# Attention with a threshold, then a two-layer feed-forward: the first nine periods of the schedule rearranged

## The chip, the cores and the metric

One core of a Trainium2 chip runs the whole program. The metric is the device time of one execution in microseconds (us). The kernel before took 487.23 us, the median of three runs (485.38 to 487.64).

## The reference

Eight batches, eight heads, 576 tokens, head size 64. For each head:

```python
scores = scale * np.matmul(q, k.transpose(0, 1, 3, 2))        # scale = 1/8
thresh = np.max(scores, axis=-1, keepdims=True) - tau
scores = np.where(scores >= thresh, scores, -1000000000.0)
attn = np.exp(scores - np.max(scores, axis=-1, keepdims=True))
attn = attn / (np.sum(attn, axis=-1, keepdims=True) + 1e-09)
x = np.matmul(attn, v)                                        # then heads side by side: 4608 x 512
h = x @ w_in                                                  # 512 -> 2048
out = np.maximum(0.01 * h, h) @ w_out                         # 2048 -> 512
```

Because a weight is kept or dropped by comparing its score with the row's maximum less 0.02, scores have to be accurate. The kernel splits each fp32 q and k into two fp16 halves, a high one and the low rest, and forms a score from three fp16 products (high x high, low x high, high x low).

## The kernel before

The work is cut into 72 *periods*. A period is four tiles of 128 queries by 576 keys: four heads of one batch and one of four interleaved blocks of query tokens (m = 0..3), in two sets of heads (so periods 0 and 1 are m = 0 of batch 0, periods 2 and 3 are m = 1, and so on); the 64 tokens left at the end of each batch form tail periods. Batch 1 begins at period 8. The loop `while n < N + PV_LAG` (line 633) writes out one period per turn, by hand: the order of the lines is the order on each engine's queue, and every queue is served in order.

What one turn n does:

- **TensorE (PE)**: `scores` (line 302) forms the four score tiles in PSUM. Then it turns q and k of later periods, turns the reciprocal sums of period n-2 (`spread`), does `pv` of period n-2 (weights times v, line 418), two halves of the feed-forward (`layer1`, `layer2`, lines 456 and 473), with `idle` matmuls in periods 0 to 3 that only keep its clock up.
- **VectorE (DVE)**: `copy_min` (line 336) four times, 0.75 us each by the profile, copies the negated scores to SBUF and takes their minimum; `weights` (line 376) makes the weights of the "plain" tiles; `evacuate` multiplies `pv` by the reciprocal sums into x.
- **ScalarE (ACT)**: `exp_plain` for the plain tiles (one instruction each), `exp_steep` for the others (two each, no work on DVE), the copies out of PSUM and the leaky relu.
- **GpSimd (POOL)**: `split_pool`, three instructions which make the fp16 halves of a pair of heads of q or k, in the period before they are turned; casts of v; DMAs that cast (`load_w` brings w_in in four parts, then w_out in four parts, fp32 to fp16 on the way); from period 5 on also the small loads (`small_at`).
- **SyncE (SP)**: the other DMAs, among them `turn_w` (line 387), a DMA transpose that turns the 128 x 2304 weights of a period for `pv`.

Three things around the change:

- *Weights turned on TensorE.* In the first periods DMA is busy with loads, so `here` (line 637) is true for the weights of periods 0, 1 and 2: in turn n+1 TensorE transposes them in three batches (6, 8 and 4 blocks of 128 columns, `turn_w_here`), and ACT, ACT and DVE copy the batches out (`take_w`). From period 3 on `turn_w` issues a DMA transpose from SP in turn n+1, and `pv` uses it in turn n+2.
- *Two ways for q and k.* The long way: POOL makes the halves (`split_at`), TensorE turns 16 fp16 pieces (`turn`), ACT and DVE copy one bank each (`take`). The short way, `unit32`: TensorE turns the fp32 values themselves, ACT takes the high half out of PSUM (`take_high`) and DVE the low one (`take_low`). Batch 0 goes the short way (its raw tiles, listed in `MIXED`, are loaded in four parts); of batch 1 three units do, in periods 5, 7 and 8.
- *A signal between the row halves.* Two pieces of a score tile pair share a PSUM bank, so one matmul of `scores` waits for a do-nothing instruction that another queue passes on once an earlier matmul is done. `SIGNAL` (line 279) names the queue: POOL in periods 0 and 1, SP in period 2, POOL in 3 to 8, SP from 9. It is queued behind all that this queue was given in the turns before.

`behind_masks` makes POOL's first work of turn n wait for the last `weights` of period n-1. Raw q and k tiles have four buffers, raw v two.

Of the kernel before, what the change touches and what calls it, by code (L numbers as in the profile page):

```python
# [33 lines left out]
def kernel(  # L34
# [10 lines left out]
    nc = tc.nc  # L45
# [30 lines left out]
            out=t[:, :, :], in_=SRC[which][b, ds(4 * s, 4), 0:MAIN, :].rearrange("h (p t) d -> p h (t d)", t=4))  # L76


    MIXED = [(0, 0, "k"), (0, 0, "q"), (0, 1, "k"), (0, 1, "q"), (1, 0, "k"), (1, 1, "q")]

    def load_part(b, s, which, h=None, t=None, eng=None):
        if (b, s, which) not in raws:
# [108 lines left out]
    def unit32(b, which, p0, np=1, t0=0, nt=4):  # L191
        return (b, which, p0, np, t0, nt)
# [64 lines left out]
    periods, first_of = [], []  # L257
# [249 lines left out]
    def at(d, n, f):  # L507
        d.setdefault(n, []).append(f)
# [68 lines left out]
    early32[1] = [[q32[0, 1]]]  # L577
    late32[1] = [q32[0, 2]]
    early32[2] = [[q32[1, 1]]]
    late32[3] = [q32[1, 2]]  # L580
    def load_w_in():

        loads = [load_w(i) for i in range(4)]
# [6 lines left out]
        at(pool_at, 1 + p // 2, lambda p=p: cast_v(0, p))  # L590
    at(pool_at, 1, lambda: cast_vtails(0))
    for i in range(4):
        at(pool_at, 1 if i < 2 else 4, lambda i=i: load_w(4 + i))

    def split_at(n, key):
        at(split_at_, n - 1, key)
# [1 line left out]


    at(loads_at, 0, lambda: load_v(0, 1))  # L600
    at(small_at, 6, lambda small: load_tails(0, "q", small=small))
    split_at(9, (0, "t", "q"))
    in_turn = [(p, w_) for p in range(NP) for w_ in "kq"]
    for b in range(1, B):
        E = 18 * (b // 2)
        if b == 1:
            units = [(0, "k", 4), (0, "q", 5), (1, "q", 6), ("t", "k", 6), (2, "k", 7), (3, "k", 8), ("t", "q", 9)]
            late32[5], late32[7], late32[8] = [unit32(1, "k", 1)], [unit32(1, "q", 2)], [unit32(1, "q", 3)]
            rows, t_at, v_at, casts = (0, 2, 4, 5), (3, 6), (4, 7, 4), (6, 7, 9, 10, 9)
        elif b % 2 == 0:  # L610
            units = [(*u, E - 8 + i) for i, u in enumerate(in_turn)] + [("t", "k", E - 5), ("t", "q", E + 9)]
            rows, t_at, v_at = (E - 11, E - 10, E - 7, E - 6), (E - 8, E + 6), (E - 5, E - 1, E - 4)
            casts = E - 1, E, E + 1, E + 2, E
        else:
            units = [(*u, E + i + i // 4) for i, u in enumerate(in_turn)] + [("t", "k", E + 4), ("t", "q", E + 9)]
            rows, t_at, v_at = (E - 3, E - 2, E + 2, E + 3), (E + 1, E + 6), (E + 1, E + 4, E + 2)
            casts = E + 3, E + 3, E + 6, E + 7, E + 5
        for p, w_, n in units:
            split_at(n, (b, p, w_))
        for i, (s, w_) in enumerate(((0, "k"), (0, "q"), (1, "k"), (1, "q"))):  # L620
            at(loads_at, rows[i], lambda b=b, s=s, w_=w_: load_main(b, s, w_))
        for w_, n in zip("kq", t_at):
            at(small_at, n, lambda b=b, w_=w_, small=nc.sync: load_tails(b, w_, small=small))
        for s in range(2):
            at(loads_at, v_at[s], lambda b=b, s=s: load_v(b, s))
        at(small_at, v_at[2], lambda b=b, small=nc.sync: load_vtails(b, small=small))
        for p in range(NP):
            at(pool_at, casts[p], lambda b=b, p=p: cast_v(b, p))
        at(pool_at, casts[4], lambda b=b: cast_vtails(b))

    N = len(periods)
    n = 0
    while n < N + PV_LAG or l1q or pending or l2q or stores:
        st = periods[n] if n < N else None
        before = periods[n - 1] if 1 <= n <= N else None
        due = periods[n - PV_LAG] if PV_LAG <= n < N + PV_LAG else None
        here = before and before.n < 3
        plain = 2 if n < 2 else 3
        keys, now32, late = turns_at.get(n, []), early32.get(n, []), late32.get(n)


        if n == 0:
            def between():
                copy_min(st, 0)
                copy_min(st, 1)
                take_low(k32[1])
                for x in now32:
                    turn32(x)
            scores(st, between)
            turn32(late)  # L650
        elif st:
            scores(st)
        bank = turn(keys) if keys else None
        for x in now32 if n else []:
            turn32(x)
        if here:
            before.wt = sb.tile([128, 2, 9, 128], FP16, tag="wT", bufs=4, name="wT")
            bank = ps.tile([128, 1024], FP16, tag="h", bufs=2, name="tp")
        if due:
            bank = spread(due, bank)  # L660
        if here:
            turn_w_here(before, 0, 6, bank[:, 0:768])
        for key in keys:
            take(key, 0, on_act)
        if due:
            take_spread(due, bank)
        for x in now32:
            take_high(x)
        if here:
            take_w(before, 0, 6, bank[:, 0:768], on_act)  # L670
        if st:
            copies(st, before, lambda: [take(key, 1, on_dve) for key in keys], now32)
            exp_plain(st, 0)
            if n == 0:
                exp_plain(st, 1)
                take_high(late)
                take_low(late)
        elif before:
            recip(before)
        work = [lambda key=key: split_pool(key) for key in split_at_.get(n, [])] + pool_at.get(n, [])  # L680
        for i, f in enumerate(work):
            mm = f()
            if i == 0 and before:
                behind_masks(mm, before)
        for key in keys:
            if key[1:] == ("t", "k"):
                widen_keys(key[0])
        if n >= 5:

            for f in small_at.get(n, []):  # L690
                f(small=nc.gpsimd)
        if n < 4:
            idle((4, 10, 8, 4)[n], spare("o"))
        if here:
            o = ps.tile([128, 1024], FP16, tag="o", bufs=1, name="wp")
            if n < 3:
                turn_w_here(before, 6, 8, o)
        elif before and st:
            turn_w(before)
        for f in loads_at.get(n, []) + (small_at.get(n, []) if n < 5 else []):  # L700
            f()
        while stores and (n >= N or n not in loads_at or len(stores) > 1):
            store()

        if due and (n == 3 or n > N):
            pv(due)
            if n > N:
                evacuate(due)
        if n == 3:
            turn_w_here(before, 6, 8, o)  # L710
            idle(12, spare("h"))
        for half in range(2):
            if half == 1 and n == 3:
                exp_steep(st, 3)
            for _ in range(2):
                if l2q:
                    layer2()
            if l1q:
                layer1()
            elif n >= N:  # L720
                settle()
            if half == 0:
                if st:
                    for i in range(1, plain if n else 0):
                        exp_plain(st, i)
                if here:
                    take_w(before, 6, 8, o, on_act)
                if late and n not in (0, 3):
                    turn32(late)
                    take_high(late)  # L730
                if n == N:

                    before.wt = sb.tile([128, 2, 9, 128], FP16, tag="wT", bufs=4, name="wT")
                    free = [(sc[:, ts(i, 512)].bitcast(FP16), 8 * i, m) for i, m in enumerate((8, 8, 2))]
                    for o, first, m in free:
                        turn_w_here(before, first, m, o)
                if due and n <= N:
                    if n != 3:
                        pv(due)
                    evacuate(due)  # L740
                if n == N:
                    a, *more = [take_w(before, first, m, o[:, 0 : 128 * m], on_dve if first else on_act)
                                for o, first, m in free]
                    for x in more:
                        tc.declare_no_dep(x.ins, a.ins, reason="other banks")
            elif st and n != 3:
                for i in range(plain, 4):
                    exp_steep(st, i)
        if n == 3:
            turn32(late)  # L750
            take_high(late)
        if here:
            o = ps.tile([128, 512], FP16, tag="o", bufs=1, name="wp")
            turn_w_here(before, 14, 4, o)
        for i in range(plain if st else 0):
            weights(st, i)
            if late and n and i == (2 if n == 3 else 0):
                take_low(late)
            if here and i == 1:
                take_w(before, 14, 4, o, on_dve)  # L760
        n += 1
# [33 lines left out]
```

## Time and profile before

| | |
|---|---|
| median of three runs | 487.23 us (485.38 to 487.64) |
| profiled execution, its own time | 485.95 us |
| its span, first to last instruction | 484.2 us |
| busy share of the span | PE 96%, DVE 89%, ACT 87%, POOL 44% |
| mean granted TensorE clock | 0.996 |
| first score matmul of periods 1 to 10 | 13.79, 21.02, 28.78, 35.50, 42.66, 49.66, 60.66, 67.67, 74.81, 81.08 us |

The difference between a line of the last row and the next is the length of a period. From period 9 on a period takes about 6.3 us, and PE and DVE are busy for all of it; so time lost or won in the first periods is found again at the end of the kernel. Period 5 runs from 42.66 to 49.66 us, period 6 from 49.66 to 60.66 us.

In the profile, "L389" is a line of the kernel; "SPq" or "POOLq" are instructions of a queue that move no data themselves, such as the issue of a DMA. A DMA's time "to landing" is from its issue to its completion signal. Times in the timeline are from the start of the span.

### The profile page before, as it was taken

What the parts mean: (1) busy time and instruction counts of PE and PEld (TensorE: products, weight loads), DVE (VectorE), ACT (ScalarE), POOL (GpSimd) and SP (SyncE); (2) the same over time, 40 slices, a digit from 0 to 9 for tenths busy, and PEclk for the clock granted to TensorE, in tenths of its full rate; (3) what the DMA queues carried; (4) which work ended last, traced back from release to release, by engine and by line L of the source; (5) the groups of instructions that cost most, each with busy time, mean ns of one, the idle gap of its engine ahead of it and who ended that gap; (6) DMA issues with size and microseconds to landing.
All of it is one profiled execution on the core that took longest, in us unless ns stands there. A gap on an engine that the chain in (4) does not pass through costs nothing.

```text
span 484.2 us, 25192 instructions
## 1 busy us (share of the span) xinstructions
PE 465.3 (96%) x10834; PEld 377.4 (78%) x10834; DVE 433.1 (89%) x1311; ACT 420.5 (87%) x781; POOL 215.0 (44%) x353
## 2 busy tenths in 40 slices
PE   7878799999999999999999999999999999999996
PEld 5667688888888888888888778888878788777774
DVE  3988789999999999999999989999999999999940
ACT  4898588999999999999999989999999899988862
POOL 2636545554465464454465574454456473000000
PEclk9999899999999999999999999999999999999999
DMA  9999987799899989789899988979899997655541
GB/s 176 233 218 189 205 189 165 153 187 199 181 177 189 237 168 173 156 164 212 178 189 192 185 188 185 151 180 192 185 184 203 193 184 123 123 122 123 123 95 45
DMA packets 206752, 83.68 MB, mean 173 GB/s; under 512 B 175792, under 2 KB 201392, under 8 KB 206640
## 3 DMA queue, kind: packets, MB, share of 16 engines
q1 hardware_dynamic: 199728, 74.79, 80.1%
q0 software_dynamic: 5504, 6.82, 7.4%
q8 instruction: 85, 1.39, 1.2%
q10 hardware_dynamic: 1408, 0.46, 0.4%
q14 instruction: 27, 0.22, 0.2%
HBM read 36.70 MB, written 9.44 MB: 95 GB/s over the span
## 4 chain that ended last, share of the span: by engine, by line
PE 87%; ACT 6%; DMA 4%; DVE 1%; issue 1%; SPq 0%; POOL 0%; POOLq 0%; ACTq 0%
PE hp L466 25%; PE o L479 25%; PE sc L297 21%; PE pv L426 8%; DMA wT<-w 4%; PE tp L410 3%; PE tp L186 3%; ACT w L373 1%; ACT e L367 1%; ACT s L372 1%; ACT wT L402 1%; PE sc L523 1%; DVE s L338 1%; ACT g L469 1%; ACT qT L232 0%
## 5 line engine op out<-in xcount | busy, mean ns | idle before, releaser
L338 DVE TENSOR_SCALAR_CACHE_REDUCE s<-sc 128x576 f32<-128x576 f32 x288 | 205.3, 753 | 17.4 <-PE sc L297 17.1
L466 PEld LDWEIGHTS <-win 128*64 128x64 f16 x4608 | 147.1, 110 | 28.8 <-DVE xt L437 1.1
L378 DVE SCALAR_TENSOR_TENSOR w<-s,th,e 128x576 f16<-128x576 f32 x214 | 164.4, 815 | 0.6 <-DVE x L445 0.2
L367 ACT ACTIVATE e<-s,mn 128x576 f16<-128x576 f32 x214 | 158.3, 778 | 0.0
L479 PE MATMUL o<-wout,g 128*64 128x512 f16 x1152 | 149.4, 381 | 0.4 <-DMA wout<-in_moe_w_out_dram 0.4
L466 PE MATMUL hp<-x,win 128*64 128x128 f16 x4096 | 137.1, 220 | 0.4 <-DVE kT L249 0.4
L469 ACT ACTIVATE g<-hp 128x512 f16<-128x512 f32 x144 | 86.1, 598 | 44.0 <-PE hp L466 43.9
L297 PE MATMUL sc<-kT,qT 64*128 64x384 f16 (+7 forms) x1920 | 120.5, 284 | 2.4 <-SPq L331 0.9
L297 PEld LDWEIGHTS <-qT 64*128 64x128 f16 (+1 forms) x1920 | 89.8, 97 | 19.7 <-SPq L331 2.0
L160 POOL TENSOR_SCALAR scaled<-raw 128x512 f32<-128x512 f32 x53 | 32.7, 616 | 148.2 <-DVE w L378 128.1
L479 PEld LDWEIGHTS <-g 128*64 128x64 f16 x1152 | 58.6, 110 | 29.6 <-issue 0.7
L171 POOL TENSOR_TENSOR half<-scaled,half 128x512 f16<-128x512 f32 (+1 forms) x68 | 71.7, 1054 | 5.8
L373 ACT ACTIVATE w<-s,minus_tau 128x576 f16<-128x576 f32 x74 | 57.4, 776 | 2.4
L372 ACT ACTIVATE s<-s,th 128x576 f32<-128x576 f32 x74 | 56.8, 767 | 0.7 <-DVE th L356 0.7
L426 PE MATMUL pv<-wT,v 128*64 128x128 f16 (+1 forms) x1600 | 53.0, 214 | 4.0 <-DMA wT<-w 2.8
L426 PEld LDWEIGHTS <-v 128*64 128x64 f16 x1600 | 45.8, 110 | 4.9 <-issue 4.0
L167 POOL CAST half<-scaled 128x512 f16<-128x512 f32 (+1 forms) x68 | 38.2, 562 | 4.4
L445 DVE TENSOR_TENSOR x<-pv,by 128x256 f16<-128x256 f32 x64 | 27.1, 424 | 8.1 <-PE pv L426 6.5
L416 ACT COPY by<-tp 128x256 f16<-128x256 f16 x72 | 26.8, 372 | 1.1 <-PE tp L397 1.1
L186 PEld LDWEIGHTS <-half 64*128 64x128 f16 x968 | 24.4, 95 | 3.5 <-DVE qT L239 1.4
L186 PE MATMUL tp<-ident,half 64*128 64x64 f16 x968 | 24.5, 190 | 1.0 <-DVE qT L239 1.0
L113 POOL CAST v<-vraw 128x256 f16<-128x256 f32 x64 | 24.0, 408 | 0.0
(61 smaller groups left out, 335.4 us busy)
## 6 DMA issues: line engine op xcount, KB each, us to landing
vraw<-in_v_dram SPq DMA_DIRECT2D x16, 512.0 KB, 5.4
out_dram<-osb SPq DMA_DIRECT2D x31, 256.0 KB, 4.0
raw<-in_q_dram SPq DMA_DIRECT2D x13, 512.0 KB, 4.9
raw<-in_k_dram SPq DMA_DIRECT2D x13, 512.0 KB, 5.1
win<-in_moe_w_in_dram POOLq DMA_DIRECT2D x4, 512.0 KB, 9.6
wout<-in_moe_w_out_dram POOLq DMA_DIRECT2D x4, 512.0 KB, 12.5
raw<-in_q_dram SPq DMA_DIRECT2D x12, 128.0 KB, 3.8
raw<-in_k_dram SPq DMA_DIRECT2D x10, 128.0 KB, 4.2
```

The lines of the kernel that those rows point to most:

```text
L171: nc.gpsimd.tensor_tensor(out=halves[key][:, 1, 0:n, :, :], in0=scaled.pop(key)[:, 0:n, :, :], in1=halves[key][:, 0, 0:n, :, :], op=AX.sub ...
L186: nc.tensor.transpose(tps[key][r][:, x, t, :], half[rows, x, t, :, :].rearrange("p h d -> p (h d)"), ident[rows, rows])
L297: yield nc.tensor.matmul(out=o, lhsT=lhs, rhs=turned[st.b, "k"][rows, kx, pair, ds(key0, n)], start=(i == 0), stop=(i == 2), skip_group_ch ...
L338: return nc.vector.tensor_scalar(out=st.s[TILES[n]][:, :], in0=sc[:, ds(PLACE[TILES[n]], 576)], scalar1=-1.0 / UNIT, scalar2=None, op0=AX. ...
L367: nc.scalar.activation(out=st.e[t][:, :], in_=st.s[t][:, :], func=AF.Exp, bias=st.mn[:, n : n + 1], scale=-1.0)
L372: nc.scalar.activation(out=z, in_=z, func=AF.Prelu, bias=st.th[:, n : n + 1], scale=-1.0, alpha=1e20)
L373: nc.scalar.activation(out=w_of(st, t), in_=z, func=AF.Exp, bias=minus_tau[:, :], scale=1.0, accum_out=st.sum[:, c, h : h + 1])
L378: st.last = nc.vector.scalar_tensor_tensor(out=w_of(st, t), in0=st.s[t][:, :], scalar=st.th[:, n : n + 1], in1=st.e[t][:, :], op0=AX.is_le ...
L426: nc.tensor.matmul(out=st.pv[ds(64 * h, 64), c, ts(u, n)], lhsT=v16[st.b % 2][:, pair, blk, :], rhs=st.wt[:, c, blk - (blk > 4), ts(u, n)] ...
L466: nc.tensor.matmul(out=hp[ds(64 * c, 64), jj, :], lhsT=w_in16[:, i, ds(128 * (4 * u + jj) + 64 * c, 64)], rhs=g.x[:, i, :], start=(i == 0) ...
L469: nc.scalar.activation(out=g.g[:, ds(4 * u, 4), :], in_=hp[:, :, :], func=AF.Prelu, bias=0.0, scale=1.0, alpha=0.01)
L479: nc.tensor.matmul(out=g.o[ds(64 * c, 64), :], lhsT=g.g[:, j, ds(64 * c, 64)], rhs=w_out16[:, j, :], start=(j == 0), stop=(j == 15), skip_ ...
```

## The change

Five things, all in the first ten periods:

1. `here` holds for periods 1 and 2 only. The weights of period 0 are turned by a DMA transpose that SP issues in turn 1. `pv` and `evacuate` of period 0 move from turn 2 to turn 3, ahead of `pv` of period 1.
2. The third and fourth part of w_out are loaded in turn 2 in place of turn 4 (the first two stay in turn 1).
3. Batch 1 goes the long way alone: the units (1, k), (2, q) and (3, q) become POOL splits for turns 5, 8 and 8, and (3, k) moves from turn 8 to 7. Its raw tiles are no longer `MIXED`, so each is loaded by one DMA.
4. The last fp32 unit of batch 0 (q tokens 2 and 3, second set of heads) moves from turn 3 to turn 4, and period 4 has two plain tiles in place of three.
5. Loads: first v of batch 1 and its small tail from turn 4 to 6, its q tail from 6 to 7, its first two v casts from turns 6 and 7 to 8; small loads of turns 5 to 8 go from POOL's queue to SP's.

```diff
-    MIXED = [(0, 0, "k"), (0, 0, "q"), (0, 1, "k"), (0, 1, "q"), (1, 0, "k"), (1, 1, "q")]
+    MIXED = [(0, 0, "k"), (0, 0, "q"), (0, 1, "k"), (0, 1, "q")]
...
-    late32[3] = [q32[1, 2]]
+    late32[4] = [q32[1, 2]]
...
-        at(pool_at, 1 if i < 2 else 4, lambda i=i: load_w(4 + i))
+        at(pool_at, 1 + i // 2, lambda i=i: load_w(4 + i))
...
-            units = [(0, "k", 4), (0, "q", 5), (1, "q", 6), ("t", "k", 6), (2, "k", 7), (3, "k", 8), ("t", "q", 9)]
-            late32[5], late32[7], late32[8] = [unit32(1, "k", 1)], [unit32(1, "q", 2)], [unit32(1, "q", 3)]
-            rows, t_at, v_at, casts = (0, 2, 4, 5), (3, 6), (4, 7, 4), (6, 7, 9, 10, 9)
+            units = [(0, "k", 4), (0, "q", 5), (1, "k", 5), (1, "q", 6), ("t", "k", 6), (2, "k", 7), (3, "k", 7), (2, "q", 8),
+                     (3, "q", 8), ("t", "q", 9)]
+            rows, t_at, v_at, casts = (0, 2, 4, 5), (3, 7), (6, 7, 6), (8, 8, 9, 10, 9)
...
-        here = before and before.n < 3
-        plain = 2 if n < 2 else 3
+        here = before and before.n in (1, 2)
+        plain = 2 if n < 2 or n == 4 else 3
...
-        if n >= 5:
+        if n >= 9:
 
             for f in small_at.get(n, []):
                 f(small=nc.gpsimd)
...
-        if due and (n == 3 or n > N):
+        if n == 3:
+
+            pv(periods[0])
+            evacuate(periods[0])
             pv(due)
-            if n > N:
-                evacuate(due)
+        elif due and n > N:
+            pv(due)
+            evacuate(due)
...
-                if due and n <= N:
+                if due and 2 < n <= N:
```

More of the change, by code (lines that the diff above doesn't have):

```diff
@@ L600 @@
     at(loads_at, 0, lambda: load_v(0, 1))
-    at(small_at, 6, lambda small: load_tails(0, "q", small=small))
+    at(small_at, 6, lambda small=nc.sync: load_tails(0, "q", small=small))
     split_at(9, (0, "t", "q"))
@@ L699 @@
             turn_w(before)
-        for f in loads_at.get(n, []) + (small_at.get(n, []) if n < 5 else []):
+        for f in loads_at.get(n, []) + (small_at.get(n, []) if n < 9 else []):
             f()
@@ L727 @@
                     take_w(before, 6, 8, o, on_act)
-                if late and n not in (0, 3):
+                if late and n:
                     turn32(late)
@@ L748 @@
                     exp_steep(st, i)
-        if n == 3:
-            turn32(late)
-            take_high(late)
         if here:
@@ L756 @@
             weights(st, i)
-            if late and n and i == (2 if n == 3 else 0):
+            if late and n and i == 0:
                 take_low(late)
```

## Prediction

> **What bounds the kernel now.** I read the table of busy time by stretch first, one stretch per period, then the chain that ended last, then the timeline of SP's queue, and last the DMA queues over short stretches. Columns of the table: length, then busy us (and instructions) of PE, weight loads, DVE, ACT, POOL; clock, DMA share, GB/s. Rows are periods 5, 6, 7, 8 and 9.
>
> ```profile
> 42.66:49.66 7.00, 6.90 (x152) 5.74 (x150) 6.47 (x19) 5.96 (x11) 3.83 (x6) 1.00 1.16 240
> 49.66:60.66 11.00, 8.20 (x155) 6.58 (x153) 8.18 (x24) 6.34 (x12) 6.12 (x10) 0.85 1.09 199
> 60.66:67.67 7.01, 6.91 (x151) 5.74 (x150) 4.92 (x15) 5.97 (x11) 3.06 (x5) 1.00 0.72 139
> 67.67:74.81 7.14, 6.88 (x151) 5.80 (x149) 6.55 (x20) 6.33 (x12) 2.91 (x6) 1.00 0.90 231
> 74.81:81.08 6.27, 6.27 (x148) 5.09 (x146) 6.27 (x21) 5.64 (x11) 4.32 (x7) 1.00 0.96 163
> ```
>
> Periods 5, 7 and 8, which carry an fp32 unit, take 7.0 to 7.1 us; period 9 without one takes 6.27, with PE and DVE full. Period 6 stands out with 11.00 us at a clock of 0.85. The chain (start, length, what) says why:
>
> ```profile
> 44.95 11.54 DMA wT<-w
> 56.49 0.14 issue
> 56.63 0.75 PE pv L426 x20
> 57.38 1.65 PE o L479 x8
> 59.02 1.71 PE hp L466 x32
> ```
>
> The transpose of period 4's weights took 11.54 us, so PE waited 2.41 us for it, and then ran a layer-2 group in 1.84 us and a layer-1 group in 1.98 (1.06 and 1.09 one period before): half speed for 3.4 us. SP's queue shows the same transpose at issue, beside the one before it:
>
> ```profile
> 36.84 2.94 SPq L389 DMA_TRANSPOSE wT<-w  x1
> 39.88 0.51 SPq L75 DMA_DIRECT2D raw<-in_k_dram  x1
> 40.49 0.55 SPq L99 DMA_DIRECT2D vraw<-in_v_dram  x1
> 44.95 7.92 SPq L389 DMA_TRANSPOSE wT<-w  x1
> ```
>
> It stood behind raw k and v, and these shared the 16 engines with the two late w_out parts (issued 39.33). How two queues share is to be seen from 30 to 33 us, where SP's k tails (256 B packets, q1) meet w_in and w_out (q0); below it, from 38.4 to 40.7 us, a transpose alone:
>
> ```profile
> q0 software_dynamic: 471, 0.47, 91.8%
> q1 hardware_dynamic: 463, 0.12, 29.7%
> ...
> q1 hardware_dynamic: 1935, 0.50, 116.7%
> ```
>
> 471 packets to 463: one for one, about 155 per us each, where a transpose alone gets 841 per us. The k tails paid for it: 11.2 us to landing at the median, against 4.1 on POOL's queue later.
>
> In periods 1 and 2 ACT is the chain; the copies of period 0's turned weights are part of it:
>
> ```profile
> 17.60 0.79 ACT L402 COPY wT<-tp 128x768 f16<-128x768 f16 x1
> 18.28 1.45 ACT L367 ACTIVATE e<-s,mn 128x576 f16<-128x576 f32 x2
> 19.62 1.00 ACT L402 COPY wT<-wp 128x1024 f16<-128x1024 f16 x1
> ```
>
> **The change, part by part** (sum against the profiled execution, 485.95 us; the median is 1.3 higher, so the same difference is added to 487.23).
>
> *Period 0's weights by DMA: what is removed.* 36 transposes on PE (0.5 + 0.6 + 0.4 us) beside ACT's chain; ACT copies of 0.79 and 1.00, one DVE copy of 0.42. ACT would end period 1 at about 23.1 instead of 24.25; DVE's copy of the last score tile (to 19.25) holds the rest. Worth 1.1 us if nothing else is late.
>
> *What is added.* SP issues a transpose at 17.45, when ACT's last weights of period 0 end (17.43). Its 2304 packets (590 KB by 256 B) start at about 18.7, behind raw k. w_in was issued at 16.68 and fills q0 from 19.2, 2048 packets of it with w_out's 1024 directly behind (q0 alone: 813 packets from 20 to 24 us). At one for one, and 143 to 155 per us, 2304 packets take 15 to 16 us: last packet at 34.0 to 34.8. The two transposes at 36.84 and 56.51 had their last two completion writes 1.1 to 1.4 us behind the others, so landing is at 36 (35.3 to 36.5). Bounds: alone, as at 36.84, it would land at 17.45 + 6.5 = 24; by the k tails' rate, 36. I take 36, since the tails are the only row with the same q0 traffic beside them.
>
> The Trainium skill (DMA: Bandwidth & Descriptors, Queues, rings and completion order) says that an engine changes rings after a whole packet of some 9 to 17 descriptors. If a transpose's 256 B records were descriptors of such packets, it would pass w_in nearly untouched, as in rival B; the k tails' records alternated singly, but no run here shows a transpose beside w_in.
>
> *Who waits.* First, `scores` of period 2 needs its signal from SP, now queued behind the issue of this transpose. That issue took 2.94 us undisturbed, and 7.92 with a full queue; the latter ended with some 1500 of its packets unserved. So the signal goes between 20.4 (no loss: the pieces before it are done about then) and 27.8 (1000 left). Before, from the signal (21.7) to `pv` of period 3 (31.26) it took 9.5 us, so a signal up to 26.5 is covered by the landing at 36; the late end, 27.8, costs 1.3. I take 25 and no cost. Raw q of batch 1 and the k tails, behind it in q1, land near 41 and 44, when POOL's splits in periods 4 and 5 want them.
>
> Second, `pv` of period 0 in turn 3, and behind it on PE `pv` of period 1, the last turned weights and layer 1. `pv` of period 1 ended at 31.98; now 36.2 + 2 x 0.75 = 37.7: **+5.7**. PE has then stood still for about 2.5 us or more, as before 56.63. Half speed on the 3.4 us that follow cost 1.7 there; here **+1.5** (0 to 1.7). By the Trainium skill (TensorE: Matmul & The Clock Gate, Part 1) the clock falls after an idle window of about 3.4 us, which is free-running; a gap of 2.5 us would then mostly cost nothing, and the sum would be 1.5 lower. The trace has 2.41 us of idling followed by half speed, but also 2.35 us before 28.43 without.
>
> *Last fp32 unit from turn 3 to 4.* Turn 3 loses 0.6 us of PE (transposes at 34.56): **-0.6**. Period 4, 7.16 before with 1.03 us of PE waiting for the DVE half of that unit, becomes like period 5 before; one plain tile less gives DVE 0.74 and costs ACT about 0.9, both inside: **-0.2** (-0.5 to +0.5).
>
> *w_out early, v later.* From period 5 on q0 is empty, so the transpose of period 4 lands as the one at 36.84 did. Period 6 goes from 11.00 to the 6.8 of a two-unit period: **-4.2** (-3.9 to -4.5). Next late would be the transpose of period 3, issued in turn 4 with some 300 to 700 w_out packets left: landing near 51.5, `pv` wants it at 52 to 54; cost 0, up to 1.
>
> *Batch 1 by fp16 halves.* In each of periods 5, 7, 8 an fp32 unit (PE 0.6, ACT 0.6, DVE 0.69) is replaced by 16 fp16 pieces (PE 0.4) and copies (ACT 0.57, DVE 0.42), DVE and PE being full: **-0.3, -0.3, -0.4**. POOL gets splits of 0.61 + 0.61 + 1.16, 2.5 us with gaps; two per turn in 4, 6, 7. Starting 1.4 us into a period, two end at 6.5 and, in turn 6, the widening copy (0.61) at 7.1. Beside DVE's weights a POOL cast took 0.98 for 0.39 (19.86), so add 0.6 to each of the last two: 8.3. POOL's signal for period 7 is wanted 0.9 into it, at 7.6: **+0.7** (0 to 1.2). DVE lost 0.12 to 0.2 per weights in such meetings: **+0.4**. The small loads that leave POOL (2.55 us in turn 6) are part of why this fits; SP issues them in about 0.6 each with slack in its queue. Casts of v in turn 8 end within the period.
>
> Sum: 5.7 + 1.5 - 0.6 - 0.2 - 4.2 - 1.0 + 0.7 + 0.4 = **+2.3 us**: 488.2 for an execution like the profiled one, 489.5 on the median.
>
> **The rivals.**
>
> A, the forecast: a new wait for period 0's transpose takes back what period 6 gives. 489.5, own range 485.7 to 493.
>
> B, the transpose is not held up by w_in and lands at 24 to 29. Then no wait in period 3: -1.1 (ACT) + 0.6 (a second `pv`) - 0.6 - 0.4 - 4.2 - 1.0 + 1.1 = -5.6: 481.6. For it: transposes have never met w_in in this trace. Against: the one-for-one rows. It decides from a landing before about 30; between 30 and 36 each us is one us.
>
> C, SP's issue holds the signal of period 2 until nearly all packets are served, at about 33. Period 2's chain of 9.5 us then starts there: `pv` at 42.5, 6 us past A, and one idling less: 494 to 495. For it: the issue of 7.92 us. Against: 1000 to 1500 packets fitted in the queue at its end.
>
> D, the change at period 6 doesn't do what it says, because the transposes of periods 3 or 4 stay late: 4 us on top of A, 493.5. Against: from 52 us on there is no q0 load.
>
> **How the numbers follow.** A 0.60, B 0.25, C and D together 0.15. A measurement of this kernel tells about 0.5% (2.4 us) from no change. A's centre lies at that bound: 0.29 slower, 0.28 same, 0.03 faster. B is all but 0.01 faster, C and D slower. Together faster 0.27, same 0.29, slower 0.44. The range reaches into B and up to C: 481 to 494.
>
> **What would show it.** Right: PE in period 3 waits several us for the DMA of wT, which lands 16 to 20 us after its issue; the SP issue of that transpose lasts over 5 us; PE waits in `scores` of period 2 for SP; period 6 shows 6.5 to 7.5 us. Wrong: the transpose lands within 8 us (B), or `scores` of period 2 starts its shared bank only after 30 (C), or period 6 still waits for wT (D).

## The result and the profile after

The changed kernel took 489.88 us (median of seven runs, 488.43 to 490.67) against 487.23 (seven runs): a ratio of 1.0053, 95% interval 1.0032 to 1.0075. That is 2.65 us slower, where 489.5 was forecast. The profiled execution has a span of 486.9 us, 2.7 more than before.

The stretches, one per period, for periods 1 to 9 of the changed kernel (length, then busy us and instructions of PE, weight loads, DVE, ACT, POOL; clock, DMA share, GB/s):

```profile
13.79:19.31 5.52, 4.25 (x51) 2.92 (x50) 5.52 (x18) 5.06 (x10) 2.79 (x4) 1.00 1.00 263
19.31:33.52 14.21, 7.09 (x83) 5.07 (x83) 7.91 (x22) 8.24 (x15) 7.98 (x15) 0.59 1.26 188
33.52:42.61 9.09, 9.09 (x170) 7.97 (x169) 6.48 (x19) 5.88 (x11) 2.38 (x3) 0.71 1.23 207
42.61:49.34 6.73, 6.22 (x145) 5.36 (x142) 6.08 (x16) 4.29 (x9) 4.75 (x6) 1.00 1.25 189
49.34:56.89 7.55, 6.79 (x164) 5.40 (x162) 6.96 (x21) 7.38 (x14) 3.83 (x6) 1.00 0.83 137
56.89:63.38 6.49, 6.42 (x155) 5.31 (x153) 6.18 (x18) 6.24 (x12) 5.05 (x7) 1.00 1.08 205
63.38:70.71 7.33, 6.73 (x163) 5.25 (x161) 7.33 (x20) 6.07 (x11) 5.52 (x7) 1.00 1.07 201
70.71:77.53 6.82, 6.59 (x163) 5.32 (x161) 6.54 (x20) 6.45 (x12) 1.47 (x3) 1.00 1.12 215
77.53:85.28 7.75, 6.47 (x147) 5.16 (x144) 7.58 (x22) 5.64 (x11) 7.28 (x13) 1.00 1.06 256
```

Periods 2 and 3 of the kernel before:

```profile
21.02:28.78 7.76, 5.19 (x106) 4.15 (x104) 6.96 (x20) 7.70 (x15) 5.06 (x11) 1.00 1.21 223
28.78:35.50 6.72, 6.72 (x156) 6.04 (x154) 5.97 (x18) 5.61 (x10) 2.38 (x3) 1.00 1.23 208
```

Period 1 is 1.7 us shorter than before (5.52 against 7.23), period 2 takes 14.21 against 7.76 and period 3 takes 9.09 against 6.72, both with a low clock (0.59 and 0.71); period 6 takes 6.49 in place of 11.00. Period 4 begins 7.1 us later than before, period 7 only 2.7 us later, and period 11 4.2 us later. The end of the kernel is 2.7 us later, so 1.5 us come back after period 11.

What PE waited for, from 14 to 92 us (total us, times, longest):

```profile
PE sc L297 <- SPq L331: 5.5, 1, 5.5
PE sc L297 <- DVE s L338: 1.6, 2, 1.3
PE wp L397 <- ACT wT L402: 1.5, 1, 1.5
PE tp L186 <- POOL half L171: 0.8, 1, 0.8
```

The great wait is the first: the scores of period 2 wait 5.5 us for the signal from SP (line 331). No `pv` waits for a turned-weights DMA. The timeline of SP's queue shows why the signal is late:

```profile
17.45 8.61 SPq L389 DMA_TRANSPOSE wT<-w  x1
26.26 0.42 SPq L75 DMA_DIRECT2D raw<-in_q_dram  x1
...
43.95 4.83 SPq L389 DMA_TRANSPOSE wT<-w  x1
...
53.19 2.72 SPq L389 DMA_TRANSPOSE wT<-w  x1
```

SP was busy with issuing period 0's transpose from 17.45 to 26.06; PE's matmul started at 26.17. The DMA queues from 25 to 35 us (packets, MB, share):

```profile
q0 software_dynamic: 1565, 1.55, 91.3%
q1 hardware_dynamic: 1564, 0.40, 32.4%
```

In ten microseconds the transpose (q1) got 1564 packets and w_in with w_out (q0) got 1565: one for one, 156 per us. The transpose landed 19.8 us after its issue, at 37.25. A stretch of 0.105 us, from 28 to 28.105, has

```profile
q0 software_dynamic: 16, 0.02, 91.4%
q1 hardware_dynamic: 16, 0.00, 31.5%
```

and the order in which the records of both queues start repeats itself every 0.105 us: one record of each queue for each of the 16 engines. The Trainium skill (DMA: Bandwidth & Descriptors, Queues, rings and completion order) has an engine change rings after a whole packet of some 9 to 17 descriptors. If the trace's 256 B records were descriptors inside such packets, they would come in runs of that length; here they alternate singly with q0's.

### The profile page after: what moved, and what is told of

Read it like the earlier page. It is cut to its first block, busy times and chain, and to the rows that moved or that the text cites. A ratio compares the mean times of both kernels' runs of the same rounds, so it can differ in the third digit from the quotient of the medians.

```text
span 486.9 us, 25198 instructions
## 1 busy us (share of the span) xinstructions
PE 465.8 (96%) x10834; PEld 377.7 (78%) x10834; DVE 435.0 (89%) x1308; ACT 419.6 (86%) x781; POOL 221.3 (45%) x358
## 4 chain that ended last, share of the span: by engine, by line
PE 87%; DVE 4%; ACT 3%; DMA 2%; SPq 1%; issue 1%; POOL 0%; DVEq 0%; POOLq 0%
PE hp L466 25%; PE o L479 24%; PE sc L297 22%; PE pv L426 8%; PE tp L410 3%; PE tp L186 3%; DVE s L338 2%; DMA rawt<-in_q_dram 1%; DMA raw<-in_k_dram 1%; ACT w L373 1%; DVE w L378 1%; SPq L389 1%; ACT e L367 1%; ACT s L372 1%; ACT g L469 0%
## 5 line engine op out<-in xcount | busy, mean ns | idle before, releaser
L378 DVE SCALAR_TENSOR_TENSOR w<-s,th,e 128x576 f16<-128x576 f32 x213 | 166.9, 831 | 0.4
L297 PE MATMUL sc<-kT,qT 64*128 64x384 f16 (+7 forms) x1920 | 121.9, 286 | 8.8 <-SPq L331 5.5
L297 PEld LDWEIGHTS <-qT 64*128 64x128 f16 (+1 forms) x1920 | 91.0, 97 | 26.1 <-SPq L331 6.2
L160 POOL TENSOR_SCALAR scaled<-raw 128x512 f32<-128x512 f32 x56 | 34.5, 616 | 144.4 <-DVE w L378 130.2
L171 POOL TENSOR_TENSOR half<-scaled,half 128x512 f16<-128x512 f32 (+1 forms) x71 | 75.5, 1063 | 6.0
L167 POOL CAST half<-scaled 128x512 f16<-128x512 f32 (+1 forms) x71 | 40.5, 570 | 4.6
## 6 DMA issues: line engine op xcount, KB each, us to landing
wout<-in_moe_w_out_dram POOLq DMA_DIRECT2D x4, 512.0 KB, 19.8
```

The source lines that it names most:

```text
L171: nc.gpsimd.tensor_tensor(out=halves[key][:, 1, 0:n, :, :], in0=scaled.pop(key)[:, 0:n, :, :], in1=halves[key][:, 0, 0:n, :, :], op=AX.sub ...
L297: yield nc.tensor.matmul(out=o, lhsT=lhs, rhs=turned[st.b, "k"][rows, kx, pair, ds(key0, n)], start=(i == 0), stop=(i == 2), skip_group_ch ...
L378: st.last = nc.vector.scalar_tensor_tensor(out=w_of(st, t), in0=st.s[t][:, :], scalar=st.th[:, n : n + 1], in1=st.e[t][:, :], op0=AX.is_le ...
```

## The experiments

**1. The signal by another queue.** Only the queue that passes on the signal of period 2 is changed.

```diff
-    SIGNAL = [nc.gpsimd, nc.gpsimd, nc.sync] + [nc.gpsimd] * 6 + [nc.sync]
+    SIGNAL = [nc.gpsimd, nc.gpsimd, nc.vector] + [nc.gpsimd] * 6 + [nc.sync]
```

> The changed kernel with one edit: the signal between the row halves in period 2 goes by VectorE's queue, not SP's. Theory (two waits stand one behind the other): the 5.5 us wait of the scores of period 2 for SP is gone, period 3 begins near 28, but the weights of period 0 still land near 37.2 (19.8 us after the issue at 17.45), so PE now waits 6 to 7 us for that DMA ahead of pv of period 0, which starts at 37.3 in place of 38.2: 488 to 489.5 us. Rival (the signal alone is the cost): pv of period 0 starts near 32 without a wait and the time falls by 5 us or more, to about 484.

Measured: 491.3 us, ratio to the kernel before 1.0073 (1.0045 to 1.0101). PE's waits from 14 to 45 us:

```profile
PE pv L426 <- DMA wT<-w: 6.1, 1, 6.1
PE wp L397 <- ACT wT L402: 2.9, 1, 2.9
PE sc L297 <- DVE s L338: 1.6, 2, 1.3
```

The wait in the scores is gone, period 3 begins at 28.05 in place of 33.52, and `pv` of period 0 then waits 6.1 us for the DMA, which landed 20.4 us after its issue. Nothing was won. The rival falls: two waits stand one behind the other, and taking away the one that the profile names leaves the other.

**2. No w_in beside the transpose.** w_in goes to turn 2, w_out to turns 2 and 3.

```diff
-    at(pool_at, 1, load_w_in)
+    at(pool_at, 2, load_w_in)
...
-        at(pool_at, 1 + i // 2, lambda i=i: load_w(4 + i))
+        at(pool_at, 2 + i // 2, lambda i=i: load_w(4 + i))
```

> The changed kernel with w_in loaded in turn 2 and w_out in turns 2 and 3, so that the transpose of period 0's weights is issued at 17.45 with no w_in beside it. Theory (one for one sharing with w_in is what made it land 19.8 us after its issue): it lands in 5 to 8 us, its issue on SP takes about 3 us, the scores of period 2 do not wait for SP, period 3 begins at 27 to 28.5 and its pv waits for nothing. The crowd then moves on: q0 is full until about 50 us, the transpose of period 3, issued near 36, lands near 52, and pv in period 5 waits some 4 to 6 us for it; 486 to 488 us in all. Rival (transposes on SP's queue are slow in the first periods for a reason of their own): the landing stays above 14 us and period 3 begins after 32.

Measured: 490.1 us, ratio 1.0064 (1.0037 to 1.0091). From the lists of DMA issues near 18 us and near 38 us (KB or count, then us to landing), and SP's timeline:

```profile
wT<-w SPq DMA_TRANSPOSE x1, 4.7
...
wT<-w SPq DMA_TRANSPOSE x1, 15.6
```

```profile
18.43 2.83 SPq L389 DMA_TRANSPOSE wT<-w  x1
...
38.20 9.83 SPq L389 DMA_TRANSPOSE wT<-w  x1
```

Without w_in beside it, the same transpose took 2.83 us to issue and landed after 4.7 us, where it had taken 8.61 and 19.8. The next one, at 38.20, met the weights instead: 9.83 us of issue, 15.6 to landing, and `pv` in period 5 waited 5.2 us. Period 5 took 14.61 us. The cause is shown, and also that w_in and w_out delay whichever transpose is issued beside them. The total was 2 us above the range expected. A part of that is the clock, which fell again in period 5 (0.77 over it): behind the wait, layer 2 and layer 1 took 1.95 us each, in place of 1.05 and 1.09 in period 4.

**3. Period 0's weights on TensorE, the rest as changed.**

```diff
-        here = before and before.n in (1, 2)
+        here = before and before.n < 3
...
-            pv(periods[0])
-            evacuate(periods[0])
             pv(due)
...
-                if due and 2 < n <= N:
+                if due and n <= N:
```

> The changed kernel with its first part undone: period 0's weights are turned on TensorE and its pv is in turn 2, as before; all else as changed. Theory (that one transpose beside w_in costs the 7 us that period 4 begins late): period 4 begins at 35 to 36 in place of 42.6, period 6 stays without the wait for wT, since the last w_out packets end near 45 and the transpose of period 3 then lands near 47.5, when pv wants it: 482 to 484 us. Rival (q0 is simply too full: w_out directly behind w_in hurts whichever transpose comes next): pv of period 3 in period 5 waits 3 us or more for its DMA, and the time is 486 or more.

> The changed kernel with period 0's weights turned on TensorE, once more, on the same chip as the kernel before with w_out moved. Its first eleven periods end 1.5 us earlier in the profiled runs, yet it took 485.9 where that one took 483.1. Theory (its waits for wT in the steady part are a matter of the DMA queues' chance order and of the chip): within 1.5 us of it, 482 to 484.5. Rival (the rest of the change, batch 1 by halves and its loads, costs time later on): again 485.5 to 486.5.

Measured: 485.92 us, ratio 0.9962 (0.9941 to 0.9984); the second time 487.51, ratio 0.9996 (0.9970 to 1.0023). In the first profile period 4 begins at 35.49, 7.1 us earlier than in the changed kernel, and period 11 at 84.12, 7.4 earlier. So the first period's transpose is worth 7 us at that point of this profile. But the end is only 1.8 us earlier in that profile, and 2 to 4 us in the medians. The rest is lost later, as PE's waits from 92 us to the end say:

```profile
PE pv L426 <- DMA wT<-w: 4.0, 4, 1.5
PE sc L297 <- SPq L331: 1.0, 2, 0.7
PE pv L426 <- ACT g L469: 0.6, 1, 0.6
```

In the second profile period 4 begins at 36.29 and period 11 at 86.69, only 4.8 us earlier than in the changed kernel. From period 3 to the end of period 6 it takes 3.5 us more than the first: 2.4 us are waits that the profile puts down to issue alone (1.6 us before line 186 in period 5), and period 3 is 1.2 us longer at a clock of 0.78, where the first profile had 1.00. After 92 us it has 2.0 us of waits for wT and 1.5 us for SP. The first result lies between its theory and its rival, and `pv` of period 3 does not wait for its DMA as the rival had it. The second lies 1 us above even its rival's range: this kernel is not within 1.5 us of the one of experiment 6.

**4. The q tail back in turn 6**, alone and with experiment 3's edit.

```diff
-            rows, t_at, v_at, casts = (0, 2, 4, 5), (3, 7), (6, 7, 6), (8, 8, 9, 10, 9)
+            rows, t_at, v_at, casts = (0, 2, 4, 5), (3, 6), (6, 7, 6), (8, 8, 9, 10, 9)
```

> The changed kernel with the q tail of batch 1 loaded in turn 6 again, not 7. Theory (the 7.75 us of period 9 come from this tail, which landed at 77.55, 7 us after its issue, and made POOL's halves late): period 9 takes 6.3 us, the time falls by 1.2 to 1.5 us to about 488.5. Rival (period 9 is long because of the casts and splits on POOL): period 9 stays at 7.5 or more, 489.5 to 490.

> Both of the former edits: period 0's weights turned on TensorE, q tail of batch 1 in turn 6. If the two costs are separate they add: 7 and 1.4 us under the changed kernel, 481 to 482.5 us, some 1 per cent under the kernel before. If the tail's lateness came from the crowded DMA queues that the first transpose leaves, the second edit gives nothing beyond the first: 483 us.

Measured: alone 489.07 us, ratio 1.0033 (1.0016 to 1.0050); with TensorE turning 486.56, ratio 0.9982 (0.9954 to 1.0011). In the changed kernel's chain the tail is to be seen (start, length, what):

```profile
71.28 6.27 DMA rawt<-in_q_dram
...
77.70 0.41 POOL scaled L160
...
80.16 0.25 PE tp L186 x4
```

Loaded in turn 6, it no longer delays POOL: period 9 falls from 7.75 to 6.46, but period 10 rises from 6.24 to 6.59, so 0.9 us are won in the profile, where 1.2 to 1.5 were expected, and about that in the medians. Its interval overlaps that of the changed kernel, so the size is not settled. Added to experiment 3's edit nothing measurable was won.

**5. Fewer DMAs in the steady part.** Output of batches 0 to 5 is not stored, with the TensorE way and in the changed kernel.

```diff
         b, m = g.where
+        if b < B - 2:
+            return
```

> The changed kernel with period 0's weights turned on TensorE and the output of batches 0 to 5 not stored (six eighths of the result are left out), so that DMA has less to move in the steady part. Theory (of the 7.4 us that the TensorE way wins by period 11, the steady part takes back 3.4, because its transposes land late when loads and stores stand before them): PE's waits for wT between 92 and 400 us fall from 4.0 to under 1 us and the time to 480 to 482. Rival (these waits do not come from the queue's load): they stay, and the time is 485 to 486.

> The changed kernel with the output of batches 0 to 5 not stored (six eighths of the result are left out); the counterpart of the TensorE way without these stores. Theory: its steady part has about 1 to 2.4 us of waits to lose, so 487.5 to 488.5; the distance between the two kernels without stores is 6.5 to 7.5 us, where it is 4.0 with stores. Rival: both fall alike, and the distance stays 4.

Measured: 483.71 us, ratio 0.9948 (0.9927 to 0.9968), and 488.70 us, ratio 1.0044 (1.0028 to 1.0060): 5.0 us apart, where the same two with stores were 2.4 to 4.0 apart. That lies between the second expectation's theory (6.5 to 7.5) and its rival (4). In the profile of the first the 4.0 us of waits for wT have shrunk, from 92 to 400 us, to

```profile
PE pv L426 <- DMA wT<-w: 0.2, 1, 0.2
```

and the profiled execution took 481.6 us, as the theory had it. The median of its four runs is 2 us higher, between theory and rival. With stores, the three profiles with TensorE turning (experiments 3 and 4) had 4.0, 2.0 and 1.3 us of such waits in the same stretch. So the profile without stores speaks for waits that depend on what the DMA queues carry; being one execution, it does not show it. That they are all of what was given back is not shown either.

**6. One part alone: w_out early in the kernel before.**

```diff
-        at(pool_at, 1 if i < 2 else 4, lambda i=i: load_w(4 + i))
+        at(pool_at, 1 + i // 2, lambda i=i: load_w(4 + i))
```

> The kernel before with one edit: the third and fourth part of w_out are loaded in turn 2, not 4. Theory (these two parts, sharing with raw k and v, made the transpose of period 4 late): period 6 takes 6.7 to 7 us in place of 11.0, and as the transpose of period 3 now meets the rest of w_out, it lands about when pv wants it (47.5): head 3.5 to 4 us shorter, the whole 483.5 to 485.5. Rival (raw k, v and the small tail, 1536 packets ahead of the transpose, are enough): period 6 stays above 9 us and the time at 487.

> The kernel before with w_out in turns 1 and 2 alone, once more, beside the two others that are to be compared with it: 483 us.

Measured: 483.14 us, ratio 0.9932 (0.9913 to 0.9950), and again 484.19, ratio 0.9933 (0.9910 to 0.9955). Periods 5 and 6, first of the first profile, then of the second:

```profile
42.96:50.99 8.03, 6.96 (x151) 5.93 (x149) 6.47 (x19) 6.07 (x11) 3.84 (x6) 1.00 1.20 220
50.99:59.15 8.16, 6.45 (x156) 5.22 (x154) 7.14 (x21) 6.24 (x12) 6.13 (x10) 1.00 1.11 179
...
43.08:50.98 7.90, 6.96 (x151) 5.94 (x149) 6.47 (x19) 6.08 (x11) 3.83 (x6) 1.00 1.19 216
50.98:61.05 10.07, 7.90 (x156) 6.24 (x154) 8.19 (x24) 6.24 (x12) 6.14 (x10) 0.85 1.12 189
```

In the first profile period 6 falls from 11.00 to 8.16 with the clock at 1.00, between the theory (6.7 to 7) and the rival (above 9). Period 5 rises from 7.00 to 8.03; 1.0 us of that is a wait before line 410 that the profile puts down to issue alone. The transpose of period 3 now meets the rest of w_out (7.64 us of issue), but lands at 47.8, before its `pv` at 48.55. What is left in period 6 is the transpose of period 4 behind raw k, v and the small tail: 8.9 us to landing, at 56.6, and `pv` starts at 56.71. In the second profile it lands 8.8 us after its issue, `pv` waits 2.2 us for it, and half speed follows as in the kernel before, so that period 6 takes 10.07 us, and periods 5 and 6 together 17.97 against 18.00 in the kernel before. That execution took 487.09 us, the longest of its twelve. This part of the change is a gain of 0.67% by itself in the medians, both times; that the gain comes from period 6 is shown by one of two profiles.

**7. And v later too.** The kernel before with w_out as in 6 and the loads of v, its tail and its first casts as in the change.

```diff
-            rows, t_at, v_at, casts = (0, 2, 4, 5), (3, 6), (4, 7, 4), (6, 7, 9, 10, 9)
+            rows, t_at, v_at, casts = (0, 2, 4, 5), (3, 6), (6, 7, 6), (8, 8, 9, 10, 9)
```

> The kernel before with all of w_out in turns 1 and 2 and, as in the change, v of batch 1 and its small tail in turn 6 and the first two casts of v in turn 8. With w_out alone moved, period 6 still took 8.16 us, because wT of period 4 stood behind raw k, v and the small tail. Theory: without v ahead, period 6 takes 6.6 to 7, and the time is 1 to 1.5 us under that kernel: 481.5 to 482.5. Rival: v in turns 6 and 7 makes a later transpose late by as much, and the time stays at 483.

Measured: 483.36 us, ratio 0.9912 (0.9883 to 0.9940), faster than both kernels; against w_out alone (0.9933 with its interval) the step is not measurable, and the 481.5 to 482.5 expected were not reached. Period 6 of its profile takes 6.49 us, as expected; period 5 takes 8.61, with a 1.6 us wait in it (45.82 to 47.37) that the profile puts down to issue alone. From 45.4 to 46.8 us the DMA engines moved 18 GB/s at most; whether the two belong together was not tried.

**8. The clock.** 88 idle matmuls before the matmul of period 2 that waits for SP.

```diff
+            if st.n == 2 and (h, x) == (0, a12) and i == 0:
+                idle(44, spare("o"))
             for mm in product(st, c, h, x, i):
```

> The changed kernel with 88 idle matmuls (5.5 us) put ahead of the matmul of period 2 that waits for SP's signal, so that PE stays busy during the wait. Theory (the half clock that followed the wait, 17 us of it in the profiled run, costs time of its own, of which the landing of wT near 37.2 leaves little to win): the clock stays at 1.0, scores of period 3 take 1.64 and not 2.99 us, pv of period 0 starts near 37.3 in place of 38.2; 1 to 2 us less, 488 to 489. Rival (periods 2 and 3 are bound by ACT and the clock does not matter): 489.5 to 490.

Measured: 490.62 us, ratio 1.0064 (1.0036 to 1.0093), no gain that can be measured. In the profile, periods 2 and 3 (19.06 to 32.11, then to 41.64):

```profile
19.06:32.11 13.05, 9.54 (x172) 8.19 (x171) 8.08 (x22) 8.03 (x15) 8.16 (x15) 1.00 1.26 173
32.11:41.64 9.53, 8.37 (x171) 7.25 (x170) 6.48 (x19) 6.50 (x11) 2.39 (x3) 0.82 1.21 216
```

The clock stays full through period 2, which is 1.2 us shorter than in the changed kernel, but is at half from 32.7 to 36.1, behind a wait of 2.8 us for ACT. `pv` of period 0 then waits 1.2 us for its DMA: half speed did cost time, and the landing takes it back. Period 4 begins 1.0 us earlier, and of that nothing is left in the median.

## Why the prediction was right, and where it was not

The total was forecast within 0.4 us, and the direction with it. The range, 481 to 494, says little by itself, since it holds rival B too. By its steps:

- *w_in and the transpose share one for one, landing near 36.* Right: 156 packets per us each, landing at 37.25; without w_in (experiment 2) the landing came 4.7 us after the issue. Rival B, a transpose that is not held up, is out.
- *The signal of period 2: "I take 25 and no cost".* The time of it was right (26.1, inside 20.4 to 27.8, after an issue of 8.61 us), the cost was wrong. From the signal to `pv` of period 3 the sum had 9.5 us, measured in the kernel before at full clock. It took 12.1, because the clock was at half from 21.8 us, 1.2 us into the 5.5 us wait, to 38.85: the scores of period 3 alone took 3.06 us in place of 1.64. With the wait filled (experiment 8) it stayed full until 32.7. So `pv` of period 0 came at 38.2, 1 us behind the landing, and the wait that ended last was the signal's, not the DMA's. Experiment 1 shows that the DMA's stood right behind.
- *`pv` of period 1 done +5.7, half clock +1.5 behind it.* The sum of the two held, the places did not. Half clock fell in periods 2 and 3 and was over 0.6 us after `pv` began, so `pv` of period 1 ended at 39.8, 7.8 us late, and behind it nothing more was lost. Period 4 was to begin 6.6 us late and began 7.1 us late. The Trainium skill (TensorE: Matmul & The Clock Gate, Part 1) has the clock return after about 3.4 us of sustained work; here PE showed 85% and 90% busy from 26.17 to 32.26 and from there to 38.85, and the clock came back only after 12.7 us. About half of the first 5 us were transposes; whether these count as work for the clock no run tries.
- *Last fp32 unit to turn 4: -0.2.* Right in period 4 (6.73 against 7.16), missed in period 5: the scores of that period need this unit, whose low half DVE finished at 50.24, so PE waited 0.6 us. The step that failed is that the wait for the DVE half goes away: it went from 1.03 to 0.6 us and moved a period on. Ahead of the low half DVE ran one `weights` of 1.53 us (lines below), 0.7 us more than usual.
- *Period 6: -4.2.* Right, at the end of its range: 6.49 against 11.00. Of the 4.5 us, w_out alone gave 2.8 and 0.9 in the two profiles of experiment 6; with the loads of v moved too (experiment 7) period 6 takes 6.49 as well.
- *Batch 1 by halves: -1.0, POOL +0.7, DVE +0.4.* Periods 5, 7 and 8 took 7.55, 7.33 and 6.82 where 7.00, 7.01 and 7.14 stood before: 0.55 longer in all, where 0.6 shorter was forecast for them without POOL's 0.7. The 0.6 us wait of the line above is in this, so without it they are as long as before. No wait of PE for POOL's signal in period 7 shows. The term that was mis-sized is DVE's +0.4, which took 0.12 to 0.2 us per `weights` beside POOL. Beside POOL's splits a `weights` took 0.7 to 0.8 us more (lines below), and DVE is busy for all 7.33 us of period 7.
- *"Casts of v in turn 8 end within the period" and the tail loads "with slack".* Missed: the q tail moved to turn 7 came behind v and raw k and landed at 77.55; the casts stood behind it on POOL's queue and ran from 80.05, in period 9; that period lost 1.5 us, of which experiment 4 wins back 0.9.
- *What is lost early is found at the end.* Only in part. By period 11 the changed kernel was 4.2 us late, not 2.3, and 1.5 us came back afterwards, as the kernel before had more waits in its steady part (1.9 us of PE's waits from 92 us on, against 0.6). The agreement at the end is thus partly luck: terms of 1 to 2 us were missed on both sides.

DVE's timeline in the changed kernel:

```profile
48.10 1.53 DVE L378 SCALAR_TENSOR_TENSOR w<-s,th,e 128x576 f16<-128x576 f32 x1
...
62.10 1.59 DVE L378 SCALAR_TENSOR_TENSOR w<-s,th,e 128x576 f16<-128x576 f32 x1
63.62 1.15 DVE L378 SCALAR_TENSOR_TENSOR w<-s,th,e 128x576 f16<-128x576 f32 x1
64.70 0.81 DVE L378 SCALAR_TENSOR_TENSOR w<-s,th,e 128x576 f16<-128x576 f32 x1
...
69.67 1.58 DVE L378 SCALAR_TENSOR_TENSOR w<-s,th,e 128x576 f16<-128x576 f32 x1
```

The four long ones start while POOL runs the third instruction of a split (line 171, 1.16 us each, from 47.86, 61.91 and 69.49) or its widening copy (from 63.02, 1.14 us). The others, at 0.80 to 0.82 us in periods 4 to 7, do not. The same four take 1.15 to 1.59 us in the profiles of experiments 3 (the first) and 8. In the kernel before no `weights` of these periods met a split, and none took more than 0.82 us. No run moves the splits alone, so this rests on the coincidence.

The part that came back after period 11 is the larger surprise. With D the part from the start of period 11 to the end of the profile, less the shortest D of all (394.6 us):

| kernel | start of period 11 | D less 394.6 | median |
|---|---|---|---|
| before | 87.31 | 2.3 | 487.2 |
| changed | 91.52 | 0.8 | 489.9 |
| changed, without stores | 92.68 | 0.0 | 488.7 |
| changed, TensorE turning (twice) | 84.12, 86.69 | 6.4, 5.7 | 485.9, 487.5 |
| the same with the q tail in turn 6 | 87.33 | 3.0 | 486.6 |
| TensorE turning, without stores | 85.03 | 0.2 | 483.7 |
| before, w_out early (twice) | 85.80, 87.85 | 1.7, 2.9 | 483.1, 484.2 |
| before, w_out early, v later | 86.34 | 0.1 | 483.4 |

From period 11 on all of them except the two without stores have the same instructions in the same order. PE's waits from 92 us on are most of D: 5.6, 4.8 and 2.4 us in the three profiles with TensorE turning. Why these kernels pay 3 to 6 us there, and the last one 0.1 from a like start, stays open. Each row is one profiled execution, and executions of one kernel differ by nearly as much (482.2 to 487.1 us in the second round of experiment 6). The medians differ beyond that: measured together, the kernel of experiment 7 (0.9883 to 0.9940) and the changed one with TensorE turning (0.9970 to 1.0023) do not overlap. Which of the other parts of the change costs this, batch 1 by halves or the loads, was not tried one by one.

## What to carry to other kernels

In these traces a DMA transpose of many small packets beside a bulk load got one packet for one, so its time was set by the number of its packets: move it out of the load's way, or turn the data on TensorE. What waits behind the issue of such a DMA on its queue, a mere signal too, waits for that issue to end, here 8.6 us of the transfer's 19.8. And before one wait is removed, look for the one that ends just behind it: here the signal and the landing were 1 us apart at `pv`, taking away the signal's alone won nothing, and taking away both let period 4 begin 7.1 and 6.3 us earlier.

## What the runs showed of the hardware

- The issue of a 2304-packet DMA transpose took 2.8 and 2.9 us of SP's queue without w_in and w_out beside it (18.43 in experiment 2, 36.84 in the kernel before), and 8.6 (changed kernel) and 9.8 us (experiment 2) beside w_in and w_out.
- PE's clock was at half for 17 us on end from 1.2 us into a wait of 5.5 us, though PE was busy for 85% or more of the last 12.7. In one kernel (experiment 3) the clock fell in period 3 behind a wait of 2.1 us in one profile, and did not behind one of 2.25 us in the other.
- DVE's `weights` took 1.53 to 1.59 us beside a POOL instruction of 1.16 us (line 171), and 0.81 us without.
- With nothing changed in the queue's order, a transpose in the steady part landed 4.5 to 9.0 us after its issue (experiment 3, first profile). In that trace's DMA records the 16 engines together move under 25 GB/s for 1 us or more 61 times between 50 and 480 us, and some 700 records of 256 B take over 1 us. Whether transfers were waiting in each of these stretches, and what causes them, was not tried.
